# Two transformer layers on one core: first shifted copies on GpSimd, and a planner that models the shared SBUF port

## The chip, the core and the metric

The program runs on one core of one Trainium2 chip. A core has five engines with a queue each: TensorE (PE, matmuls, with its weight loads shown apart as PEld), VectorE (DVE), ScalarE (ACT), GpSimd (POOL) and SyncE (SP, which issues the DMAs here). Each engine takes its instructions in the order of its queue; between engines semaphores set the order. The metric is the device time of one execution in microseconds (us), lower is better. The median of three executions is compared.

## What is computed

Input is x, 1 x 2048 x 512 in bfloat16. An attention block with 32 heads of 16 channels and a dense block with 1792 hidden channels are applied, then both a second time with the same weights.

```python
def _A_ref(x, wqkv, wo):
    qkv = (x @ wqkv).reshape(B, S, 3, H, Dh).transpose(2, 0, 3, 1, 4)
    q, k, v = qkv[0], qkv[1], qkv[2]
    scores = jnp.einsum("bhqd,bhkd->bhqk", q, k) * (Dh ** -0.5)
    p = _softmax(scores, axis=-1)
    o = jnp.einsum("bhqk,bhkd->bhqd", p, v)
    return o.transpose(0, 2, 1, 3).reshape(B, S, D) @ wo

def _B_ref(x, w1, b1, w2, b2):
    h = _gelu(jnp.einsum("bsd,df->bsf", x, w1) + b1)
    return jnp.einsum("bsf,fd->bsd", h, w2) + b2

x = x + _A_ref(_layernorm(x), A_wqkv, A_wo)
x = x + _B_ref(_layernorm(x), B_w1, B_b1, B_w2, B_b2)
x = x + _A_ref(_layernorm(x), A_wqkv, A_wo)
x = x + _B_ref(_layernorm(x), B_w1, B_b1, B_w2, B_b2)
```

The exponentials are the bulk of the elementwise work: 2 layers x 32 heads x 2048 x 2048 scores.

## The kernel before

**Cells.** The scores are made in cells of 128 keys x 512 columns of (query, head), one PSUM bank each. There are 4096 cells. They are grouped in passes: a pass is one layer, one chunk of 512 queries (a "segment"; the last chunk of layer 1 is cut in two), one group `g` of heads, and a list of key tiles. In a pass with all 16 key tiles there are 64 cells, since each key tile has four cells `a`, one for each 32-row group of TensorE.

**Two ways to take an exponential.** Most cells go to ScalarE, which reads two or three PSUM banks in one Exp (line 1466, `exps`). The cells of four key tiles of each layer (`KD`, line 45) may go to VectorE instead; let us call such a cell a d-cell. For a d-cell `dfirst` (line 1283) turns the score into a 16-bit integer whose bits are, read as bfloat16, a coarse power of two. To make the power accurate, the sum over four copies is used, whose integers are shifted by 0, 32, 64 and 96. They are weighted by copies of V that GpSimd has scaled (`VC`, line 1068, weights `VW`). So a d-cell takes four PV matmuls (one with V, three with VC) where a cell of ScalarE takes one.

**The chain of a pair.** d-cells are evacuated into a buffer `du`, which holds two of them (four buffers), one of them (one buffer, `dh` in the trace), or two in a piece of `kt` that is free in layer 1. When both cells of a buffer are in, `dchain` (line 1332) makes the shifted copies: line 1344 makes copy 1 from copy 0 for all cells of the buffer at once (the first shifted copy, 128 x 1024 for two cells), and line 1346 makes copies 2 and 3 from copies 0 and 1 (the second shifted copy, 128 x 2048). Both are VectorE instructions here, and they read and write SBUF. Then the PV matmuls read the four copies, and the buffer is free again.

**Who gets a d-cell.** `attach` (line 1215) adds d-cells to a matmul group that makes scores for ScalarE. It needs a free bank (6 or 7, which the projections and the dense layers use as well), a free `du` buffer, and a bank whose last reader will be done in time. `swap` (line 1192) gives a bank of ScalarE's own to VectorE when VectorE is not more than 0.5 us behind. `solo` (line 1291) makes one alone. Whatever d-cells are left when a pass has no others go to ScalarE (`next_act`). So the number of d-cells isn't fixed: it is what the planner finds room for.

**The planner.** Everything else follows from a list scheduler written in the kernel (`_Sched`, lines 208 to 390), which runs when the program is built. Each step of work is an `_Op` with an engine and a price in us. Generators (threads with a priority) yield ops, and ask for slots of named pools (`acq`, `take`, `rel`). The planner keeps a clock for each engine, picks the op that can start first (or, among ready ones, the one of the best priority), and appends it to its engine's queue. So the order in every queue is fixed when the program is built, from these prices; on the chip only the semaphores move the work. A thread's code between two ops runs as soon as the op before has been placed.

**Around the change.** `norm` (line 718) ends a pass: it adds the parts, transposes the sums to `XT`, takes the reciprocal of the row sums to `RC`, multiplies to `OTT` (on GpSimd for most passes, line 754) and transposes back to `OTN`. `passes` (line 1003) sets the order of passes: in layer 1 the first chunk's eight passes and `EARLY` passes of the second chunk run first over 12 key tiles, and then over the last 4, whose keys come from the last chunk of layer 0. A pass cut in two needs a copy (line 734) and an add (line 739) of VectorE in place of one transpose from PSUM. `free` (line 1090) chooses a PSUM bank for filler matmuls[...], among banks 0 to 7; bank 5 (`PVB`) collects the PV sums. GpSimd otherwise makes masked queries (`qpad`, line 1085), layer norm outputs (line 602), reciprocal roots (line 588) and VC.

Of the kernel before, what the change touches and what calls it, by code (L numbers as in the profile page):

```python
# [5 lines left out]
ALU = mybir.AluOpType  # L6
# [25 lines left out]
DU = 9  # L32
# [8 lines left out]
PACE = {(1, 2): (0.03, 0.05, 0.36, 0.02), (1, 3): (0.05, 0.07, 0.55, 0.1)}  # L41
JB = 0.64
JS = 0.025
EARLY = 4
KD = ((4, 5, 6, 7), (0, 1, 2, 12))
NKD = 4
TAIL = 10
# [12 lines left out]
COLD = 8  # L60
DPRIO = 9
CPRIO = 8
FPRIO = 1.5
PVP = 2
PTURG = 6
# [9 lines left out]
SHIFT = 32  # L75
# [126 lines left out]
        self.done = False  # L202


LATENCY = {"pe": 0.20, "act": 0.10, "dve": 0.10, "pool": 0.15, "sp": 0.1}


class _Sched:
# [5 lines left out]
    def __init__(self, P):  # L214
        self.P = P
        self.clock = {e: 0.0 for e in P.ENGS}
        self.end = {}
        self.pools = {}
        self.tokens = {}
        self.threads = []  # L220
        self.nseq = 0
        self.mode = "F"
        self.ops = []
        self.stream = []
        self.filler, self.free, self.fills = None, None, set()

    def pool(self, name, slots):
        self.pools[name] = list(slots)
# [66 lines left out]
    def _prio(self, op):  # L295
        return op.prio() if callable(op.prio) else op.prio

    def landed(self, keys):
        return max(self.end.get(self.P.lastw[k], 0.0) if k in self.P.lastw else 1e9 for k in keys)

# [33 lines left out]
    def run(self):  # L334
        while True:
            moved = True
            while moved:
                moved = False
                for th in list(self.threads):
                    if self._advance(th):  # L340
                        moved = True
            self.threads = [t for t in self.threads if not t.done]
            best = {}
            for th in self.threads:
                if th.op is None:
                    continue
                e = th.op.eng
                rdy = self._ready(th.op)
                if rdy is None:
                    continue  # L350
                best.setdefault(e, []).append((th, rdy))
            if not best:
                if self.threads:
                    raise RuntimeError("stuck: %r" % [(t.prio, t.block) for t in self.threads])
                return
            pick = None
            for e, cand in best.items():
                now = self.clock[e]
                nowc = [c for c in cand if c[1] <= now]
                if nowc:  # L360
                    ch = min(nowc, key=lambda c: (self._prio(c[0].op), c[0].seq))
                else:
                    ch = min(cand, key=lambda c: (c[1], self._prio(c[0].op), c[0].seq))
                start = max(now, ch[1])
                stop = start + self._cost(ch[0].op)
                for c in cand:
                    if c[0].op.slack is not None and c is not ch and c[1] + c[0].op.slack < stop:
                        ch = c
                        start = max(now, ch[1])
                        break  # L370
                if pick is None or start < pick[0]:
                    pick = (start, e, ch[0])
            start, e, th = pick
            op = th.op
            th.op = None
            if op.late is not None:
                op.late(op, start)
            if e == "pe":
                mode = self.mode
                self.fill(start, op)  # L380
                if mode != self.mode:
                    start = max(self.clock["pe"], start - SW * (op.mode != self.mode) + SW * (op.mode != mode))
            ev = self.P.group(e, op.fns, op.reads, op.writes, op.sem, op.by)
            cost = self._cost(op)
            if e == "pe":
                self.mode = op.mode
                self.note(start + cost - op.cost, start + cost, op)
            self.ops.append((e, start, cost, op.writes[0] if op.writes else ""))
            self.clock[e] = start + cost
            self.end[ev] = start + cost + op.tail + LATENCY[e]  # L390

# [110 lines left out]
class _Plan:  # L502
# [215 lines left out]
    def norm(self, l, seg, g, b, part, final):  # L718

        T = self.T  # L720
        pv = self.bank(b)
        key = "B.%d" % b
        qc, q0, w = seg
        if qc == 0:
            pt, pk = T["PART"][l][:, g, :], "PART.%d.%d" % (l, g)
            over = ["V0.%d" % k for k in range(self.NT)] + ["V01"] if l else []
        else:
            pt, pk = T["PART1"][:, g, :], "PART1.%d" % g
            over = ["K0.%d.%d" % (g // 2, c) for c in range(self.NQ)]
        prev = self.before(l, seg)  # L730
        if final and prev:
            yield ("need", ("ofree",) + prev)
        if not final:
            yield _Op("dve", DV, lambda e: e.tensor_copy(pt, pv), reads=[key], writes=[pk] + over)
            yield ("rel", "pv", b)
            return
        xt = T["XT"]
        if part:
            yield _Op("dve", DV, lambda e: e.tensor_tensor(out=pt, in0=pt, in1=pv, op=ALU.add), reads=[key, pk], writes=[pk])
            yield ("rel", "pv", b)  # L740
            yield _Op("dve", 0.7, lambda e: e.transpose(xt[:, :], pt), reads=[pk], writes=["XT"])
        else:
            yield _Op("dve", 0.7, lambda e: e.transpose(xt[:, :], pv), reads=[key], writes=["XT"])  # L743
            yield ("rel", "pv", b)
        x3 = xt[:, :].rearrange("p (k c) -> p k c", c=32)
        yield _Op("dve", 0.23, lambda e: e.reciprocal(T["RC"][:, :].rearrange("p (k o) -> p k o", o=1), x3[:, :, 16:17]),  # L746
                  reads=["XT"], writes=["RC"])
        gb, ts = self.heads(seg, g)
        o = gb % 2
        pool = g < 6 and seg[2] == 512  # L750
        nb = w // 32
        for i, t in enumerate(ts):
            o3 = T["OTT"][:, o, 0:w].rearrange("p (k c) -> p k c", c=32)[:, :, 16 * t:16 * t + 16]
            yield _Op(*(("pool", 0.1 + 0.55 * w / 512) if pool else ("dve", 0.1 + 0.31 * w / 512)), lambda e, i=i, o3=o3: e.tensor_tensor(  # L754
                out=o3, in0=x3[:, i * nb:i * nb + nb, 0:16],
                in1=T["RC"][:, i * nb:i * nb + nb, None].to_broadcast([128, nb, 16]), op=ALU.mult),
                reads=["XT", "RC"], writes=["OTT.%d.%d" % (o, t)])
        if ts[-1] == 1:
            yield _Op("dve", 0.05 + 0.65 * w / 512, lambda e: e.transpose(T["OTN"][:, gb, q0:q0 + w], T["OTT"][:, o, 0:w]),
                      reads=["OTT.%d.0" % o, "OTT.%d.1" % o],  # L760
                      writes=["OTN.%d.%d" % (gb, t % 4) for t in self.tiles(seg)])
            yield ("give", ("otn", l, seg, gb))

    def heads(self, seg, g):
# [325 lines left out]
    def free(self, now, ahead):  # L1090
        P = self.P
        best = (None, 1e9)
        src = self.source()
        for b in (6, 7, 0, 1, 2, 3, 4, 5) if src else ():
            k = "B.%d" % b
            if k in ahead or b in self.hold or k in P.lastw and not P.reads.get(k) and P.lastw[k] not in self.s.fills:
                continue
            t = max([0.0] + [self.s.end.get(ev, 0.0) + FOLD for ev in P.deps(src, [k]) if ev[0] != "pe"])
            if max(t, now) < max(best[1], now):
                best = (b, t)  # L1100
        k = "B.%d" % PVB
        if best[1] > now and self.pvopen and "VC.0.0" in P.lastw and k not in ahead:
            best = (PVB, 0.0)
        return best
# [227 lines left out]
    def dchain(self, pair):  # L1332
# [5 lines left out]
        if self.open is pair:  # L1338
            self.open = None
        yield ("cond", lambda: pair.get("done", 0) == len(cells))  # L1340
        n = len(cells)
        U = T["DU"][du]
        key = [["DU.%d.%d.%d" % (du, i, j) for j in range(n)] for i in range(4)]
        yield _Op("dve", 0.08 + 0.14 * n, lambda e: e.tensor_scalar(U[:, 1, 0:n, :], U[:, 0, 0:n, :], SHIFT, None, op0=ALU.add),  # L1344
                  reads=key[0], writes=key[1])
        yield _Op("dve", 0.08 + 0.28 * n, lambda e: e.tensor_scalar(U[:, 2:4, 0:n, :], U[:, 0:2, 0:n, :], 2 * SHIFT, None, op0=ALU.add),  # L1346
                  reads=key[0] + key[1], writes=key[2] + key[3])
        self.duleft[du] = n
        for jj, (pi, kt, a) in enumerate(cells):
            l, seg, g = self.pas[pi][:3]  # L1350
            gb, ts = self.heads(seg, g)
# [208 lines left out]
    def run(self):  # L1560
        s = self.s
        self.phase = {}
        s.pool("misc", MISC)
        s.pool("dbank", [])
        s.route = self.route
        s.pool("pv", [PVB])
        s.pool("s", range(len(SLOTS)))
# [54 lines left out]
```

The softmax here doesn't subtract the row's maximum and nothing guards it: scores larger than these inputs give would overflow.

## Time and profile before

| What | Value |
|---|---|
| median of three executions | 1588.41 us (1587.63 to 1589.98) |
| the profiled execution | 1589.16 us, span of its instructions 1587.3 us |
| granted TensorE clock, mean | 0.995 |
| GpSimd busy | 200.5 us in 250 instructions |
| cells on ScalarE / on VectorE | 3207 / 889 |
| first shifted copies | 391 of two cells, 107 of one cell |
| first Exp starts, last Exp ends | 12.6 us, 1560.8 us |

The cells are counted from the forms of lines 1466 and 1283. A row of a group gives its line, engine and operation, what it writes and reads, its shapes and count, its busy time in us, the mean of one in ns, and the idle time of the engine just before it with what ended most of that. Busy time is a union: overlapping instructions count once. In a table by stretches of time, the count in brackets stands beside the busy us of each engine.

### The profile page before, as it was taken

The numbers are of one execution on the slowest core, as the hardware profiler recorded it, in microseconds if no ns is written. First come the engines' busy times: TensorE is split into PE (matmuls) and PEld (weight loads), VectorE is DVE, ScalarE is ACT, GpSimd is POOL, SyncE is SP. The second block draws the span as 40 slices with busy tenths as digits, with TensorE's granted clock in tenths as the row PEclk, the third lists the DMA queues.
The fourth block names the chain that finished last, engine by engine and source line by source line (L and its number), as shares of the span: only waits on it lengthen the run. The fifth ranks groups of instructions, "written<-read, shape, count | busy, mean of one in ns | idle before, by whom it ended". The sixth has DMA issues, their size and how long they took to land.

```text
span 1587.3 us, 42896 instructions
## 1 busy us (share of the span) xinstructions
PE 1424.2 (90%) x18701; PEld 444.6 (28%) x18701; DVE 1352.0 (85%) x2564; ACT 1547.1 (97%) x1393; POOL 200.5 (13%) x250
## 2 busy tenths in 40 slices
PE   8998888899999898988989998888998889898988
PEld 3222222222222222222222222222222222333344
DVE  5689999888898889978788789899878988998984
ACT  7999999999999999999999999999999999999996
POOL 5200012001100201002120020122001000010000
PEclk9999999999999999999999999999999999999999
DMA  5100001241114311143111510001251105312520
GB/s 140 22 2 1 2 14 41 77 132 46 27 45 130 85 41 28 42 140 74 36 28 48 172 44 28 1 2 33 67 167 43 28 15 151 103 36 87 155 82 29
DMA packets 141767, 96.88 MB, mean 61 GB/s; under 512 B 36877, under 2 KB 141582, under 8 KB 141582
## 3 DMA queue, kind: packets, MB, share of 16 engines
q1 hardware_dynamic: 141582, 94.14, 21.2%
q8 instruction: 149, 2.44, 0.6%
q14 instruction: 36, 0.29, 0.1%
HBM read 84.41 MB, written 2.10 MB: 55 GB/s over the span
## 4 chain that ended last, share of the span: by engine, by line
ACT 67%; PE 29%; DVE 2%; POOL 1%; issue 1%; DMA 0%; ACTq 0%; POOLq 0%
ACT pt L1466 60%; PE ps L512 11%; PE ps L1137 9%; PE ps L1527 8%; ACT g L893 3%; ACT v L1466 2%; ACT kt L1466 1%; ACT q L1466 1%; DVE du L1283 1%; ACT L893 1%; ACT L1466 0%; DMA xf<-xln 0%; PE ps L1125 0%; POOL xln L602 0%; POOL rstd L588 0%
## 5 line engine op out<-in xcount | busy, mean ns | idle before, releaser
L1466 ACT ACTIVATE pt<-ps 128x1536 bf16<-128x1536 f32 (+2 forms) x1261 | 1384.2, 1246 | 15.2 <-PE ps L1137 10.3
L1137 PE MATMUL ps<-qp,kt 32*128 32x512 bf16 x4096 | 538.0, 385 | 140.8 <-ACT pt L1466 106.7
L1283 DVE TENSOR_SCALAR du<-ps 128x512 uint16<-128x512 f32 x711 | 479.7, 685 | 97.5 <-PE ps L1137 89.6
L1527 PE MATMUL ps<-pt,v 128*17 128x512 bf16 (+1 forms) x3368 | 433.8, 359 | 2.3 <-ACT pt L1466 0.8
L1527 PE MATMUL ps<-du,vc 128*17 128x512 bf16 (+1 forms) x2394 | 333.8, 358 | 2.7 <-DVE du L1346 1.4
L1137 PEld LDWEIGHTS ps<-qp,kt 32*128 32x128 bf16 x4096 | 140.6, 91 | 685.9 <-ACT pt L1466 304.2
L1346 DVE TENSOR_SCALAR du<-du 128x2048 uint16<-128x2048 uint16 x361 | 246.3, 687 | 2.5
L1085 POOL TENSOR_SCALAR qp<-q,mask 128x512 bf16<-128x512 bf16 (+1 forms) x91 | 66.3, 728 | 1013.8 <-PE ps L1137 1005.1
L512 PE MATMUL ps<-xf,wr 128*32 128x512 bf16 (+1 forms) x2400 | 170.8, 368 | 1.7 <-DMA xf<-xln 1.1
L1527 PE MATMUL ps<-du,v 128*17 128x512 bf16 (+1 forms) x798 | 154.7, 360 | 1.7 <-DVE xt L743 0.9
L1344 DVE TENSOR_SCALAR du<-du 128x1024 uint16<-128x1024 uint16 x361 | 150.5, 428 | 2.0
L1527 PEld LDWEIGHTS ps<-pt,v 128*17 128x17 bf16 x3368 | 111.8, 89 | 113.0 <-issue 72.9
L512 PE MATMUL ps<-wr,g 128*32 128x512 bf16 x1600 | 123.8, 384 | 5.5 <-ACT g L893 5.0
L1527 PEld LDWEIGHTS ps<-du,vc 128*17 128x17 bf16 x2394 | 92.5, 89 | 62.7 <-issue 27.5
L872 DVE TENSOR_SCALAR g<-ps,hb1t 128x512 bf16<-128x512 f32 (+1 forms) x112 | 79.8, 713 | 13.8 <-PE ps L512 12.9
L1527 PE MATMUL ps<-dh,vc 128*17 128x512 bf16 (+1 forms) x321 | 90.6, 358 | 0.0
L1283 DVE TENSOR_SCALAR dh<-ps 128x512 uint16<-128x512 f32 x96 | 65.8, 685 | 11.5 <-PE ps L1137 10.8
L1283 DVE TENSOR_SCALAR kt<-ps 128x512 uint16<-128x512 f32 x82 | 56.1, 684 | 20.7 <-PE ps L1137 19.9
L512 PEld LDWEIGHTS ps<-xf,wr 128*32 128x32 bf16 x2400 | 53.6, 95 | 61.5 <-issue 33.5
L602 POOL TENSOR_SCALAR xln<-x,rstd,nmr 128x512 bf16<-128x512 bf16 x58 | 58.2, 1008 | 33.3 <-DMA xf<-xln 23.2
L754 POOL TENSOR_TENSOR ott<-xt,rc 128x256 bf16<-128x256 f32 x42 | 29.5, 703 | 178.5 <-DVE rc L746 178.5
L1125 PE MATMUL ps<-vc 128*32 128x512 bf16 x476 | 50.9, 395 | 0.1
(93 smaller groups left out, 1185.2 us busy)
## 6 DMA issues: line engine op xcount, KB each, us to landing
wr<-in_B_w_dram SPq DMA_DIRECT2D x256, 256.0 KB, 2.9
wr<-in_A_wqkv_dram SPq DMA_DIRECT2D x24, 256.0 KB, 2.9
wr<-in_A_wo_dram SPq DMA_DIRECT2D x18, 256.0 KB, 2.9
out_dram<-x SPq DMA_DIRECT2D x16, 128.0 KB, 2.7
g<-in_A_wqkv_dram SPq DMA_DIRECT2D x3, 512.0 KB, 5.1
x<-in_A_x_dram SPq DMA_DIRECT2D x3, 512.0 KB, 8.0
q<-in_B_w_dram SPq DMA_DIRECT2D x3, 512.0 KB, 3.9
kt<-in_B_w_dram SPq DMA_DIRECT2D x4, 256.0 KB, 3.3
```

Of the source, the lines that this page charges most:

```text
L512: return [lambda e, a=a: e.matmul(out[32 * a:32 * a + 32, :], lhsT=lhsT[:, 32 * a:32 * a + 32], rhs=rhs, start=start, stop=stop, tile_posi ...
L602: yield _Op(eng, cost, lambda e: e.tensor_scalar(T["XLN"][:, x, :], T["X"][:, t, :], T["RSTD"][:, t:t + 1], T["NMR"][:, t:t + 1], op0=ALU. ...
L872: yield _Op("dve", 0.21 + n / 966, lambda e, fc=fc, pb=pb: e.tensor_scalar(T["G"][:, fc, q], pb, T["HB1T"][:, fc:fc + 1], None, op0=ALU.ad ...
L893: lambda e, g=g: e.activation(out=g, in_=g, func=ACT.Gelu_apprx_tanh), reads=gk, writes=gk, prio=2)
L1085: yield _Op("pool", 0.1 + 0.6 * w / 512, lambda e, s=s, q=q, i=i, t=t, w=w: e.tensor_scalar(T["QP"][:, s, w * i:w * i + w], q, T["MASK"][: ...
L1125: fns.append(lambda e, o=o, w=w, a=a, m=m: e.matmul(o, lhsT=w, rhs=rhs, start=start, stop=start, tile_position=(0, m * a)))
L1137: return (lambda e: e.matmul(o, lhsT=lhsT, rhs=rhs, start=True, stop=True, tile_position=(32 * a, 0)), ["K%d.%d.%d" % (l, gb, kt // 4), "Q ...
L1283: yield _Op("dve", 0.68, lambda e: e.tensor_scalar(u, self.bank(b), E_SCALE, E_BIAS, op0=ALU.mult, op1=ALU.add), reads=["B.%d" % b], write ...
L1344: yield _Op("dve", 0.08 + 0.14 * n, lambda e: e.tensor_scalar(U[:, 1, 0:n, :], U[:, 0, 0:n, :], SHIFT, None, op0=ALU.add), reads=key[0], w ...
L1346: yield _Op("dve", 0.08 + 0.28 * n, lambda e: e.tensor_scalar(U[:, 2:4, 0:n, :], U[:, 0:2, 0:n, :], 2 * SHIFT, None, op0=ALU.add), reads=k ...
L1466: yield _Op("act", 0.065 + 0.4267 * n, lambda e, src=src, dst=dst: e.activation(out=dst, in_=src, func=ACT.Exp, scale=0.25), reads=["B.%d" ...
L1527: op.fns.append(lambda e, o=o, lhsT=q[0][0][m], rhs=q[0][1][:, n * m:n * m + n], a=a, st=st, sp=sp: e.matmul(o, lhsT=lhsT, rhs=rhs, start= ...
```

## The change

The first shifted copy of a buffer goes to GpSimd if, when its last evacuation has been placed, GpSimd's clock in the plan is less than `SPARE` = 0.3 us past VectorE's; else VectorE makes it as before. The planner prices it at 0.1 us + 0.65 us for each cell there. The second copy stays on VectorE (`WHOLE` is False). The planner also keeps the last four stretches in which each of the two engines holds the port to SBUF that they share: on GpSimd every op but the reciprocal root, on VectorE the shifted copies and the quick layer norm output. `unlocked` moves an op's ready time to the end of such a stretch of the other engine, unless VectorE follows closely on a locking op of its own.

Four edits come with it. `EARLY` goes from 4 to 2. `norm` takes a slot for `XT` and for its half of `OTT`, and gives them back when they have been read. Bank 5 is no longer in the list that `free` runs over (it still takes zero-weight fillers by the rule below that list). The prices of other ops are as before.

```diff
-EARLY = 4
+EARLY = 2
...
+SPARE = 0.3
+WHOLE = False
...
+HOLD = (0.05, 0.13)
...
+    def locking(self, op):
+        w = op.writes[0] if op.writes else ""
+        if op.eng == "pool":
+            return not w.startswith("RSTD")
+        return op.eng == "dve" and (w.startswith("XLN") or w.startswith("DU") and w.split(".")[2] != "0")
+
+    def unlocked(self, op, rdy):
+        if op.eng not in self.locks or not self.locking(op):
+            return rdy
+        now = t = max(rdy, self.clock[op.eng])
+        for a, b in self.locks["pool" if op.eng == "dve" else "dve"]:
+            if a <= t < b and not (op.eng == "dve" and a >= self.fast[0] and t < self.fast[1] + 0.02):
+                t = b
+        return t if t > now else rdy
...
-                best.setdefault(e, []).append((th, rdy))
+                best.setdefault(e, []).append((th, self.unlocked(th.op, rdy)))
...
+            if self.locking(op):
+                self.fast = (start, start + cost) if e == "dve" else self.fast
+                self.locks[e] = self.locks[e][-3:] + [(start + HOLD[0], start + cost - HOLD[1])]
...
+        gb, ts = self.heads(seg, g)
+        yield ("acq", "xt")
         if part:
...
+        if ts[0] == 0:
+            yield ("take", ("ott", o))
...
+        yield ("rel", "xt", 0)
         if ts[-1] == 1:
...
+            yield ("rel", "ott", o)
...
-        for b in (6, 7, 0, 1, 2, 3, 4, 5) if src else ():
+        for b in (6, 7, 0, 1, 2, 3, 4) if src else ():
...
-        yield _Op("dve", 0.08 + 0.14 * n, lambda e: e.tensor_scalar(U[:, 1, 0:n, :], U[:, 0, 0:n, :], SHIFT, None, op0=ALU.add),
+        clock = self.s.clock
+        eng, fix, one = ("pool", 0.1, 0.65) if clock["pool"] < clock["dve"] + SPARE else ("dve", 0.08, 0.14)
+        yield _Op(eng, fix + one * n, lambda e: e.tensor_scalar(U[:, 1, 0:n, :], U[:, 0, 0:n, :], SHIFT, None, op0=ALU.add),
                   reads=key[0], writes=key[1])
-        yield _Op("dve", 0.08 + 0.28 * n, lambda e: e.tensor_scalar(U[:, 2:4, 0:n, :], U[:, 0:2, 0:n, :], 2 * SHIFT, None, op0=ALU.add),
+        eng, fix, one = ("pool", 0.1, 0.65) if eng == "pool" and WHOLE else ("dve", 0.08, 0.14)
+        yield _Op(eng, fix + 2 * one * n, lambda e: e.tensor_scalar(U[:, 2:4, 0:n, :], U[:, 0:2, 0:n, :], 2 * SHIFT, None, op0=ALU.add),
                   reads=key[0] + key[1], writes=key[2] + key[3])
```

More of the change, by code (lines that the diff above doesn't have):

```diff
@@ L225, in __init__ @@
         self.filler, self.free, self.fills = None, None, set()
+        self.locks = {"pool": [], "dve": []}
+        self.fast = (0.0, 0.0)
     def pool(self, name, slots):
@@ L747, in norm @@
                   reads=["XT"], writes=["RC"])
-        gb, ts = self.heads(seg, g)
         o = gb % 2
+        if ts[0] == 0:
+            yield ("take", ("ott", o))
         pool = g < 6 and seg[2] == 512
@@ L1564, in run @@
         s.pool("dbank", [])
+        s.pool("xt", [0])
+        s.pool("ott", [0, 1])
         s.route = self.route
```

## The prediction

> **What bounds the kernel now.** I read the busy line first, then the chain of waits, the groups, and last the table of stretches of 40 us.
>
> ```profile
> span 1587.3 us, 42896 instructions
> PE 1424.2 (90%) x18701; PEld 444.6 (28%) x18701; DVE 1352.0 (85%) x2564; ACT 1547.1 (97%) x1393; POOL 200.5 (13%) x250
> ...
> ACT 67%; PE 29%; DVE 2%; POOL 1%; issue 1%; DMA 0%; ACTq 0%; POOLq 0%
> ...
> L1466 ACT ACTIVATE pt<-ps 128x1536 bf16<-128x1536 f32 (+2 forms) x1261 | 1384.2, 1246 | 15.2 <-PE ps L1137 10.3
> ```
>
> ScalarE is busy 97% of the span, and in front of its main row of Exps it idled 15.2 us in all. First Exp to last is 12.6 to 1560.8 us; what lies outside (a start, and a tail of 26.5 us on the last dense block) isn't touched by the change. So the time falls only if ScalarE gets fewer cells, or rises if it has to wait. Its 1547.1 us less everything that isn't Exp on scores (gelu 43.9 + 3.3, table loads 10.3 + 9.0 + 1.3, casts and others 13.8) leave 1465.5 us for 3207 cells: 0.457 us a cell. Each cell that VectorE takes in addition is worth that much.
>
> What then limits VectorE's share, 889 cells of the 1024 that its key tiles hold?
>
> ```profile
> 160.00:200.00 40.00, 32.41 (x364) 8.74 (x363) 37.77 (x74) 39.99 (x36) 3.02 (x4) 1.00 0.01 2
> 680.00:720.00 40.00, 35.78 (x470) 11.00 (x470) 27.63 (x50) 39.88 (x32) 1.34 (x3) 1.00 0.53 154
> 880.00:920.00 40.00, 36.72 (x483) 10.88 (x485) 30.17 (x53) 39.80 (x37) 1.39 (x2) 1.00 0.55 158
> 1240.00:1280.00 40.00, 35.12 (x439) 10.20 (x437) 37.61 (x69) 39.87 (x37) 2.94 (x4) 1.00 0.08 21
> ```
>
> The columns are PE, PEld, DVE, ACT, POOL busy. There are two kinds of stretch. Where dense work is thin, VectorE is busy 37 to 38 of 40 us: it is full. Where weights stream (DMA share 0.5) it is busy 28 to 30, and TensorE and the two banks shared with the dense layers set the limit. Of the 38 stretches from 40 to 1560 us, 23 have VectorE at 35 us or more: 60%. GpSimd is nearly idle in both kinds.
>
> ```profile
> L1283 DVE TENSOR_SCALAR du<-ps 128x512 uint16<-128x512 f32 x711 | 479.7, 685 | 97.5 <-PE ps L1137 89.6
> L1346 DVE TENSOR_SCALAR du<-du 128x2048 uint16<-128x2048 uint16 x350 | 241.2, 693 | 2.5
> L1344 DVE TENSOR_SCALAR du<-du 128x1024 uint16<-128x1024 uint16 x350 | 147.9, 433 | 2.0
> L1085 POOL TENSOR_SCALAR qp<-q,mask 128x512 bf16<-128x512 bf16 x75 | 56.4, 752 | 854.6 <-PE ps L1137 846.6 <-ACT q L669 7.9
> ```
>
> With the smaller forms, the first copies (L1344) are 195 us, the second ones (L1346) 317 us and the evacuations 889 x 0.685 = 609 us. A d-cell costs VectorE 1.26 us. I also paired each copy with its evacuations in the order of the records: from the end of the last evacuation to the start of the first copy a chain waits 3.0 us in the median (3.5 mean), since evacuations go first, and from the first copy's end to the second's start 0.64 us. Buffers stand full in that wait.
>
> **What the Trainium skill says.** "SBUF — State Buffer", section "Who interferes with whom": GpSimd shares a pair of ports with VectorE's two-port modes, and whoever starts first holds it for the whole instruction while the other blocks. The trace agrees; at 190.97 us a GpSimd op started first, and a copy that has 684 ns in the median took 1.05 us:
>
> ```profile
> 190.97 0.69 POOL L1085 TENSOR_SCALAR qp<-q,mask 128x512 bf16<-128x512 bf16 x1 [8.42 <-PE ps L1137]
> ...
> 191.15 1.05 DVE L1346 TENSOR_SCALAR du<-du 128x2048 uint16<-128x2048 uint16 x1
> ```
>
> "VectorE: DVE Perf Modes", section "The perf-mode tier table": a 16-bit tensor_scalar in SBUF runs at 4x, 693 ns for 2048 elements, and PSUM sources run slower. Our rows have 693 for 2048 and 685 for 512 from PSUM, so the copies are two-port and the evacuations, which overlap GpSimd without getting longer (690 ns either way), are not. "GPSIMD Engine Reference", section 4.1: one-input elementwise work is roughly line rate there. Undisturbed, line 1085 has 694 ns for 512 elements and 482 for 256, so 0.83 ns an element.
>
> **The change, part by part.**
>
> First copies that move. A buffer goes to GpSimd unless GpSimd is booked over 0.3 us past VectorE. Chains start 3.0 us apart in the mean, a quarter of the gaps under 0.8 us; a copy books 1.4 us, and GpSimd's other work holds 13%. I estimate that 65% go: 254 of the 391 pairs and 70 of the 107 singles. That takes 254 x 0.43 + 70 x 0.28 = 129 us from VectorE. EARLY = 2 takes two pairs of copy and add, 4 x 0.69 = 2.7 us more.
>
> Their price on GpSimd. No row has a 16-bit integer add there. From below: line 1068 has 646 ns undisturbed for 544 elements, so 646 + 480 x 0.83 = 1.04 us for 1024. From above: two of line 1085 with its disturbances, 1.50 us, and more if integers are converted in more steps. I take the planner's 1.4 us (0.75 for one cell), as it lies inside. GpSimd gets 254 x 1.4 + 70 x 0.75 = 408 us, so about 610 us, 38%. Queued behind such a copy are qpad, layer norm outputs and OTT products; they are made for passes ahead or for work with a pass's length of slack (about 25 us), so 1.4 us there costs nothing. If that cover fails, it is 1.4 us on a chunk's dense block, some ten times.
>
> The port. Now 36 of the 996 copies are over 0.12 us longer than their median, 13 us in excess. With GpSimd busy three times as long, ops 1.6 times as long, and 670 two-port copies left of 996, this gives 13 x 3 x 1.6 x 0.67 = 42 us for a plan blind to the port, and nothing if the plan evades every clash. I take 20.
>
> New d-cells. Net relief is 129 + 3 - 20 = 112 us. A d-cell then costs 0.685 + 0.357 + about 0.09 = 1.13 us, so 99 cells if VectorE were the only limit. It is in 60% of the time: 60 cells. In the other stretches banks and TensorE hold, and I take a third of the remaining 39: 13. So 73 cells, within the 135 left. Gain on ScalarE: 73 x 0.457 = 33 us. The copy's wait of 3.0 us also goes, for about 0.2 + 1.4 us on GpSimd, so buffers come free no later than now.
>
> What they add. 3 more PV matmuls for each, 219 in all, beside 944 filler matmuls (two rows of L1125, 476 and 468) that exist only to fill TensorE's gaps; they replace those. But VectorE's and GpSimd's queues now wait on each other, and a late copy delays evacuations behind it, then the scores' bank, then an Exp. ScalarE's waits could stay at 15.2 us or double; I take 10 more.
>
> EARLY also takes 2 x 48 cells out of the stretch that covers the last chunk's keys of layer 1. The last of them (L683) lands at 953 us, and the passes over them would start at cell 2528, which was scored at 972 us: 19 us in hand, so nothing; if the cover were gone, ScalarE would wait for as much as is missing. XT and OTT slots bind passes 25 us apart, and the removed bank is one of eight for fillers: nothing each.
>
> Sum: -33 + 10 = -23, and 1589.2 - 23 = 1566 for the profiled execution. The median shown is 0.8 us below that execution: 1565.
>
> **Rivals.** (a) Forecast: 15 to 80 more d-cells, 1579 to 1546; chance 0.62. (b) The freed time turns idle, because banks, buffers and TensorE limit d-cells everywhere: evacuations already idle 97.5 us waiting for TensorE, which speaks for it; VectorE at 37.8 of 40 us speaks against. 10 more cells less 5 us of waits: 1588; chance 0.15, half of it within 0.2%. (c) Nearly all 135 cells go over, with no more waits: 1589 - 135 x 0.457 = 1527, or 1540 for 105; needs the dense stretches to gain as well; 0.07. (d) Slower: the GpSimd copy takes longer than planned. The second copy stands in VectorE's fixed queue and waits for it, with all evacuations behind. In full stretches there are 324 x 0.6 = 195 such chains; the 0.64 us that now lie between the copies cover half, so each us of mean lateness costs 97 us. Against the 23 us gained it decides from 0.24 us, a pair's copy of 1.64 us. At 1.8 us it costs 39 us: 1589 - 23 + 39 = 1605. For it speaks that no trace shows the integer op there; against it the undisturbed 0.83 ns an element. Chance 0.16, one part of it within 0.2%. That the change does nothing is excluded by GpSimd's idleness, which meets its condition at almost any time.
>
> **Numbers.** A measurement here can tell 0.2%, 3 us, from no change. Faster: 0.62 + 0.08 + 0.07 = 0.77; same 0.08; slower 0.15. The range leaves 0.06 below 1545 (c) and some 0.13 above 1592 (d).
>
> **What would show it.** Right: some 320 tensor_scalar adds on GpSimd near 1.4 us (1.1 for clean ones); 940 to 980 evacuations of line 1283; Exp time down about 33 us; ACT still at 96 to 97%; second copies with few over 0.9 us; d-cells up in the full stretches and little elsewhere. Wrong: a GpSimd copy of 1.7 us or more, VectorE idle before second copies with GpSimd as the releaser, or d-cells up and ScalarE's share down by as much.

## The result and the profile after

| | before | after |
|---|---|---|
| median of four | 1588.66 us | 1881.16 us |
| ratio, 95% interval | | 1.184 (1.182 to 1.186) |
| d-cells, of 4096 cells | 889 | 927 |
| first copies on GpSimd | 0 of 498 | 492 of 519 |
| granted TensorE clock | 0.995 | 0.929 |

The kernel became 18% slower; 1565 us was forecast. The page after, in the order used before: busy time, the chain of waits, the groups that matter.

```profile
span 1879.3 us, 43405 instructions
PE 1535.6 (82%) x18877; PEld 448.0 (24%) x18877; DVE 1365.2 (73%) x2148; ACT 1560.4 (83%) x1388; POOL 1488.6 (79%) x740
...
POOL 59%; DVE 23%; PE 15%; issue 1%; ACT 1%; DMA 0%; SPq 0%; DVEq 0%
...
L1497 ACT ACTIVATE pt<-ps 128x1024 bf16<-128x1024 f32 (+1 forms) x1257 | 1393.9, 1195 | 271.0 <-PE ps L1165 254.2
```

ScalarE was 67% of the chain and is 1%; GpSimd was 1% and is 59%. ScalarE now idles 271 us in front of the Exps where it idled 15. Its busy time is 13 us longer although it has 38 cells fewer. Before, the durations of its Exps, added one by one, are 1669 us, and the time that they cover is 1467 us: back to back they overlap. After they add to 1599 and cover 1480, since the waits leave less to overlap. ScalarE is idle for 318.9 us of the span against 40.2, which is 279 us more. These 279 and the 13 are the whole 292 us.

The groups by form show why: the GpSimd copies, and VectorE's second copies, which were 693 ns.

```profile
L1374 POOL TENSOR_SCALAR du<-du 128x1024 uint16<-128x1024 uint16 x360 | 1025.3, 2857 | 245.6 <-DVE du L1311 240.4 <-DVE varr L609 4.1
L1374 POOL TENSOR_SCALAR dh<-dh 128x512 uint16<-128x512 uint16 x79 | 129.3, 1636 | 13.6 <-DVE dh L1311 13.5
...
L1377 DVE TENSOR_SCALAR du<-du 128x2048 uint16<-128x2048 uint16 x366 | 348.1, 958 | 194.3 <-POOL du L1374 193.8
```

A copy of 1024 elements takes 2.86 us in the mean (2.77 in the median), where the planner has 1.40 and my bounds were 1.04 and 1.50. VectorE idles 194 us in front of this group of second copies for GpSimd, and each takes 265 ns longer than before. GpSimd's own queue, from the timeline, shows that the delay adds up:

```profile
599.51 5.50 POOL L1374 TENSOR_SCALAR du<-du 128x1024 uint16<-128x1024 uint16 x2 [1.41 <-DVE du L1311]
604.98 1.62 POOL L1374 TENSOR_SCALAR dh<-dh 128x512 uint16<-128x512 uint16 x1
606.57 2.76 POOL L1374 TENSOR_SCALAR du<-du 128x1024 uint16<-128x1024 uint16 x1
```

Three copies of two cells and one of a single cell follow without a gap, 9.8 us of work that the plan has as 4.95. On VectorE in the same stretch:

```profile
605.05 1.09 DVE L1377 TENSOR_SCALAR du<-du 128x2048 uint16<-128x2048 uint16 x1 [0.62 <-POOL du L1374]
606.63 1.25 DVE L1377 TENSOR_SCALAR dh<-dh 128x1024 uint16<-128x1024 uint16 x1 [0.50 <-POOL dh L1374]
607.80 0.68 DVE L1311 TENSOR_SCALAR du<-ps 128x512 uint16<-128x512 f32 x1
609.37 0.69 DVE L1377 TENSOR_SCALAR du<-du 128x2048 uint16<-128x2048 uint16 x1 [0.89 <-POOL du L1374]
```

Each second copy first stands in the queue until its first copy is done, and the first two then take far longer than their 0.69 and 0.43 us, because the next GpSimd copy has begun. The evacuation at 607.80, with its bank of scores, comes after both. That is the rival (d) of the prediction, at a size it didn't have. In all, VectorE idles 291 us waiting for GpSimd, where it idled 2.4 us before.

The lines show one thing more. The second copy at 606.63 began 0.06 us after a GpSimd copy and ended 1.45 us before it: GpSimd did not hold the port for the whole of its 2.76 us. A second copy that began later in a GpSimd copy wasn't held up at all:

```profile
1436.56 2.77 POOL L1374 TENSOR_SCALAR du<-du 128x1024 uint16<-128x1024 uint16 x1
...
1437.53 0.68 DVE L1377 TENSOR_SCALAR du<-du 128x2048 uint16<-128x2048 uint16 x1
```

I take the GpSimd copies of two cells in this trace that were not delayed themselves. The 61 second copies that began in the first 0.1 us of one took 0.81 to 0.89 us longer than normal. The 20 that began between 0.9 and 1.7 us into one took no longer than normal. In the run `e2_priced` below, 13 that began 1.8 to 2.5 us into one were held again, until 2.63 to 2.67 us after its start. So the prediction's sentence, that whoever starts first holds the port "for the whole instruction", does not fit the slow copy, and the planner, which books the port for nearly the whole of a copy, has it wrong there. For the fast copy of `e5_mult_add` below it nearly fits: six second copies were held until 0.91 us after the start of a copy of 1.05 us.

### The profile page after: what moved, and what is told of

It is laid out like the page before. It is cut to its first block, busy times and chain, and to the rows that moved or that the text cites. A ratio compares the mean times of both kernels' runs of the same rounds, so it can differ in the third digit from the quotient of the medians.

```text
span 1879.3 us, 43405 instructions
## 1 busy us (share of the span) xinstructions
PE 1535.6 (82%) x18877; PEld 448.0 (24%) x18877; DVE 1365.2 (73%) x2148; ACT 1560.4 (83%) x1388; POOL 1488.6 (79%) x740
## 4 chain that ended last, share of the span: by engine, by line
POOL 59%; DVE 23%; PE 15%; issue 1%; ACT 1%; DMA 0%; SPq 0%; DVEq 0%
POOL du L1374 44%; DVE du L1311 7%; DVE du L1377 7%; PE ps L535 6%; POOL kt L1374 4%; PE ps L1558 4%; POOL dh L1374 4%; PE ps L1165 4%; POOL qp L1113 2%; POOL xln L625 2%; DVE g L900 1%; ACT pt L1497 1%; DVE kt L1311 1%; DVE dh L1377 1%; POOL ott L780 1%
## 5 line engine op out<-in xcount | busy, mean ns | idle before, releaser
L1497 ACT ACTIVATE pt<-ps 128x1024 bf16<-128x1024 f32 (+1 forms) x1257 | 1393.9, 1195 | 271.0 <-PE ps L1165 254.2
L1374 POOL TENSOR_SCALAR du<-du 128x1024 uint16<-128x1024 uint16 (+1 forms) x370 | 1041.6, 2824 | 247.0 <-DVE du L1311 241.8
L1165 PE MATMUL ps<-qp,kt 32*128 32x512 bf16 x4096 | 556.8, 405 | 178.3 <-DVE du L1311 86.7
L1377 DVE TENSOR_SCALAR du<-du 128x2048 uint16<-128x2048 uint16 (+1 forms) x379 | 356.7, 949 | 196.8 <-POOL du L1374 196.2
L1558 PE MATMUL ps<-pt,v 128*17 128x512 bf16 (+1 forms) x3317 | 478.1, 379 | 26.3 <-POOL du L1374 9.7
L1558 PE MATMUL ps<-du,vc 128*17 128x512 bf16 (+1 forms) x2511 | 375.6, 390 | 35.5 <-DVE du L1377 18.7
L1374 POOL TENSOR_SCALAR kt<-kt 128x1024 uint16<-128x1024 uint16 (+1 forms) x43 | 119.3, 2775 | 29.3 <-DVE kt L1311 29.2
L1374 POOL TENSOR_SCALAR dh<-dh 128x512 uint16<-128x512 uint16 x79 | 129.3, 1636 | 13.6 <-DVE dh L1311 13.5
L900 DVE TENSOR_SCALAR g<-ps,hb1t 128x512 bf16<-128x512 f32 (+1 forms) x112 | 79.1, 706 | 10.5 <-PE ps L535 10.3
L1377 DVE TENSOR_SCALAR dh<-dh 128x1024 uint16<-128x1024 uint16 x96 | 61.8, 644 | 18.9 <-POOL dh L1374 18.8
L1558 PE MATMUL ps<-kt,vc 128*17 128x512 bf16 (+1 forms) x324 | 60.7, 371 | 5.3 <-DVE du L1377 3.2
```

Source lines behind the costliest of these rows:

```text
L900: yield _Op("dve", 0.21 + n / 966, lambda e, fc=fc, pb=pb: e.tensor_scalar(T["G"][:, fc, q], pb, T["HB1T"][:, fc:fc + 1], None, op0=ALU.ad ...
L1165: return (lambda e: e.matmul(o, lhsT=lhsT, rhs=rhs, start=True, stop=True, tile_position=(32 * a, 0)), ["K%d.%d.%d" % (l, gb, kt // 4), "Q ...
L1374: yield _Op(eng, fix + one * n, lambda e: e.tensor_scalar(U[:, 1, 0:n, :], U[:, 0, 0:n, :], SHIFT, None, op0=ALU.add), reads=key[0], write ...
L1377: yield _Op(eng, fix + 2 * one * n, lambda e: e.tensor_scalar(U[:, 2:4, 0:n, :], U[:, 0:2, 0:n, :], 2 * SHIFT, None, op0=ALU.add), reads=k ...
L1497: yield _Op("act", 0.065 + 0.4267 * n, lambda e, src=src, dst=dst: e.activation(out=dst, in_=src, func=ACT.Exp, scale=0.25), reads=["B.%d" ...
L1558: op.fns.append(lambda e, o=o, lhsT=q[0][0][m], rhs=q[0][1][:, n * m:n * m + n], a=a, st=st, sp=sp: e.matmul(o, lhsT=lhsT, rhs=rhs, start= ...
```

## Experiments: what makes the copy slow

Two questions were open. Why does the copy take 2.77 us, when other tensor_scalar rows on GpSimd have 0.83 ns an element? And is the loss the slow copy as such, or a plan made with half its price? The first batch:

`e1_two_ops`, the copy as two additions on GpSimd:

```diff
-tensor_scalar(U[:, 1, 0:n, :], U[:, 0, 0:n, :], SHIFT, None, op0=ALU.add)
+tensor_scalar(U[:, 1, 0:n, :], U[:, 0, 0:n, :], SHIFT, 0.0, op0=ALU.add, op1=ALU.add)
```

> The changed kernel, with the GpSimd copy written as two operations (add 32, add 0) instead of one; same plan, same order of every queue. In the changed kernel the copy of 1024 elements took 2.77 us in the median, 2.5 ns an element, where the planner has 1.40; the two-operation rows on bfloat16 have 0.83 ns an element. Theory A (the form with one operation is what is slow): the copy falls to 1.0 to 1.3 us and the kernel to 1560 to 1575 us, since the plan is then kept. Theory B (16-bit integers are slow on GpSimd): the copy stays at 2.7 us or gets longer, the kernel stays at 1880 us or above.

`e4_bf16_view`, the same bytes as bfloat16:

```diff
-tensor_scalar(U[:, 1, 0:n, :], U[:, 0, 0:n, :], SHIFT, None, op0=ALU.add)
+tensor_scalar(U[:, 1, 0:n, :].bitcast(BF16), U[:, 0, 0:n, :].bitcast(BF16), SHIFT, None, op0=ALU.add)
```

> The changed kernel, with the GpSimd copy (one operation, as it is) reading and writing the same bytes as bfloat16 instead of uint16, so that copy 1 holds other values; only its time is of interest. Theory A (one-operation form slow): still 2.5 ns an element, 2.7 us. Theory B (integer type slow): 0.8 to 0.9 ns an element, 1.0 to 1.2 us for 1024, and the kernel at 1560 to 1580 us.

Measured: two additions 2217.4 us (ratio 1.397, 1.394 to 1.399), the copy 3.63 us in the median (the 3.67 in the texts below is the mean). The bfloat16 view, one execution: 1885.7 us. Its row, from the view of the buffer's tile (shortest, median and longest in ns):

```profile
L1375 POOL TENSOR_SCALAR du<-du x370: 1485/2770/3581, 68.5 to 1847.2; 128x1024 bf16<-128x1024 bf16 x177, 128x512 bf16<-128x512 bf16 x8
```

To the nanosecond the same median as with uint16. So theory B, the integer type, is out, and theory A in its form of then ("one operation is slow, two are fast") is out as well: a second addition made it slower. What is left is the kind of operation. The fast rows of before are line 1085 (times mask, times 1.0), line 1068 (times weight, times 1.0) and line 602 (times, plus): two operations, at least one of them a multiplication. Line 602 has a single form, 0.77 us for 512 elements, so its time for one element isn't known, though the first text below counts it in. Three runs separate the number of operations, the multiplication and its place. `e5_mult_add` has

```diff
-tensor_scalar(U[:, 1, 0:n, :], U[:, 0, 0:n, :], SHIFT, None, op0=ALU.add)
+tensor_scalar(U[:, 1, 0:n, :], U[:, 0, 0:n, :], 1.0, SHIFT, op0=ALU.mult, op1=ALU.add)
```

on GpSimd, `e6_mult_alone` has `1.0, None, op0=ALU.mult`, and `f4_add_mult` has `SHIFT, 1.0, op0=ALU.add, op1=ALU.mult`. In all of them, and in the two runs above, each queue has the same instructions in the same order as in the changed kernel, since the planner's prices aren't touched.

> The changed kernel, plan and queues as they are, with the GpSimd copy written as times 1.0, plus 32 in place of plus 32. One add took 2.77 us for 1024 elements, on uint16 and on the same bytes as bfloat16 alike, and two adds 3.67 us; the rows on GpSimd that begin with a multiplication (masked queries, scaled V, layer norm outputs) have 0.83 ns an element. Theory E (it is the pair of operations that decides: multiply first is fast, add first is slow): the copy takes 1.0 to 1.25 us, below the planner's 1.40, and the kernel 1560 to 1580 us, faster than before. Theory F (anything on these buffers is slow on GpSimd, by place or integer values): 2.8 us or more, the kernel at 1880 us or above.

> As the run with times 1.0, plus 32, but with the multiplication by 1.0 alone, so that copy 1 holds what copy 0 holds; only its time is of interest. If one operation alone is slow as such, the copy takes 2.7 us here and the kernel 1880 us; if the add as first operation is what is slow, it takes 1.0 to 1.25 us and the kernel 1560 to 1580 us.

> As the run with times 1.0, plus 32, with the two operations the other way round: plus 32, times 1.0; same values. If it is a multiplication as first operation that is fast on GpSimd, this takes over 2.7 us a copy (two adds took 3.67 us) and the kernel 1880 us or more. If any pair with a multiplication is fast, it takes 1.05 us and the kernel 1584 us.

The row of the copy with times 1.0, plus 32, and then that of times 1.0 alone:

```profile
L1375 POOL TENSOR_SCALAR du<-du x370: 616/1047/1522, 68.2 to 1548.1; 128x1024 uint16<-128x1024 uint16 x177, 128x512 uint16<-128x512 uint16 x8
```

```profile
L1375 POOL TENSOR_SCALAR du<-du x370: 1485/2770/3577, 68.6 to 1843.0; 128x1024 uint16<-128x1024 uint16 x177, 128x512 uint16<-128x512 uint16 x8
```

| operations on GpSimd | 1024 elements, median us | kernel, us |
|---|---|---|
| plus 32 (the change) | 2.77 | 1881.2 |
| plus 32, on bfloat16 | 2.77 | 1885.7 (one execution) |
| times 1.0 | 2.77 | 1880.8 (one execution) |
| plus 32, plus 0 | 3.63 | 2217.4 |
| times 1.0, plus 32 | 1.05 | 1584.3 |
| plus 32, times 1.0 | 1.05 | 1580.2 (one execution) |

A pair with a multiplication in either place takes 1.05 us, one operation alone 2.77, two additions 3.63. So theory E has the right time for times 1.0, plus 32, but not the right reason: the single multiplication is as slow as the single addition, and the order of the pair makes no difference. The kernel with that pair is also 4 us above the 1560 to 1580 us that the theory gave it. From the undisturbed forms of 512 and 1024 elements, the pair has (1047 - 621) / 512 = 0.83 ns an element, one operation (2770 - 1489) / 512 = 2.50, two additions (3628 - 1921) / 512 = 3.33. Why a pair with a multiplication is faster was not found out, and other operations or other constants than 1.0 weren't run in the copy.

With the pair, the same queues that gave 1881 us give 1584.3 us: ratio 0.9967 to the kernel before (0.9957 to 0.9977). So in this plan the duration of this one instruction is the whole loss, and the rest of the change, the move to GpSimd included, gains a little.

## Experiments: the plan, and the other edits

`e2_priced` leaves the slow copy and tells the planner its price.

```diff
-eng, fix, one = ("pool", 0.1, 0.65) if clock["pool"] < clock["dve"] + SPARE else ("dve", 0.08, 0.14)
+eng, fix, one = ("pool", 0.22, 1.275) if clock["pool"] < clock["dve"] + SPARE else ("dve", 0.08, 0.14)
```

> The changed kernel, with the planner's price for the GpSimd copy set to what was measured (0.22 + 1.275 us a cell, 2.77 us for two) and nothing else. Theory C (the time was lost because the plan was made with a price of half: queues in the wrong order): the kernel falls to 1590 to 1630 us, waits of ScalarE for scores from 271 to under 60 us, and the d-cells fall below 889. Theory D (the shared port itself costs it, whatever the plan): the second copies on VectorE stay at 950 ns, and the kernel stays above 1750 us.

It ran in 1633.5 us (ratio 1.028, 1.027 to 1.030), 3.5 us above the range of theory C and far below that of theory D. The busy time of the engines, and the groups of the second copies and of the main Exps, by form:

```profile
PE 1457.4 (89%) x18809; PEld 451.7 (28%) x18809; DVE 1285.4 (79%) x2134; ACT 1568.7 (96%) x1401; POOL 1075.3 (66%) x573
```

```profile
L1377 DVE TENSOR_SCALAR du<-du 128x2048 uint16<-128x2048 uint16 x336 | 272.5, 821 | 14.6 <-POOL du L1374 14.4
```

```profile
L1497 ACT ACTIVATE pt<-ps 128x1024 bf16<-128x1024 f32 x749 | 786.1, 1091 | 4.9 <-PE ps L1165 2.6 <-PE ps L1558 1.7
L1497 ACT ACTIVATE pt<-ps 128x1536 bf16<-128x1536 f32 x506 | 765.3, 1512 | 28.4 <-PE ps L1558 15.2 <-PE ps L1165 11.1
```

The copies are as slow as ever, yet VectorE waits 15 us for them instead of 194, and ScalarE 33 us instead of 271. The second copies are down from 958 to 821 ns, so the port costs less in this plan too, though not nothing (693 before). The plan finds 844 d-cells, 45 fewer than before; ScalarE's busy time is 21.6 us longer than before (45 x 0.457 = 21), and its idle time 22.3 us longer. So of the 292 us, 248 go when the price in the plan is true, with the instruction unchanged. But this plan also sends only 325 copies to GpSimd in place of 492. How much of the 248 us comes from the order of the queues, and how much from a third fewer slow copies, wasn't separated.

`e7_mult_add_priced` does the reverse: the fast pair, and the planner's price lowered from 1.40 to the undisturbed time.

```diff
-eng, fix, one = ("pool", 0.1, 0.65) if clock["pool"] < clock["dve"] + SPARE else ("dve", 0.08, 0.14)
+eng, fix, one = ("pool", 0.2, 0.43) if clock["pool"] < clock["dve"] + SPARE else ("dve", 0.08, 0.14)
```

> Times 1.0, plus 32 as before, with the planner's price for it set to 0.2 + 0.43 us a cell (1.06 us for two), the undisturbed figure of line 1068 taken to 1024 elements. Theory E: the copy at that time, chains shorter, 15 to 40 more d-cells than before, 1560 to 1580 us and within 6 us of the run that keeps the old price. Theory F: slower than the run with the old price, since the plan is then further from the chip.

1599.8 us, ratio 1.0067 (1.0046 to 1.0087): slower than with the price that is too high, and outside what theory E expected. Theory F has the direction right, but not its reason: the copies of two cells take 1.11 us in the mean. This plan has 906 d-cells, not 927. In the profiled executions, 1592.9 us against 1586.1 with the old price, the cells account for all of it: ScalarE is busy 8.5 us longer (21 x 0.457 = 10), and idle 1.7 us less. VectorE does idle longer before the second copies, 25.6 us against 10.5, but that did not reach ScalarE there. The other half of the 15 us between the medians goes with a lower granted clock: four of the six executions had 0.981 to 0.986 and took 1598.0 to 1603.6 us, the two with 0.991 took 1592.9 and 1595.7, and those of `e5_mult_add` with 0.991 took 1585.6 and 1585.9. Whether this plan brings the lower clock about isn't shown.

The other edits. `e3_all_dve` is the change with `SPARE = -1e9`, so that no copy moves. `f1_all_dve_early4` has `EARLY = 4` besides. `k1_slots_bank` also takes the port out of the planner (`locking` returns False for both engines).

> The changed kernel with SPARE = -1e9, so that no copy goes to GpSimd; EARLY = 2, the slots for XT and OTT, the bank list and the port in the planner stay. If the GpSimd copies are the whole loss, this is at the time before, 1583 to 1594 us (my steps for the four other edits were nothing and 3 us of VectorE). If one of them costs (keys of the last chunk late at EARLY = 2, above all), it is 1600 us or more.

> No copy on GpSimd (as the run with SPARE = -1e9, 1594.7 us, 0.37% above before) and EARLY back at 4. If EARLY = 2 is what cost those 6 us, this is at the time before, 1586 to 1591 us. If the port in the planner, the slots or the bank list cost them, it stays at 1593 to 1597 us.

> No copy on GpSimd, EARLY = 4 and the port out of the planner: of the change only the slots for XT and OTT and the bank list are left. With the port this was 1597.4 us, 0.46% above before. If the planner's port cost those 8 us, this is at the time before, 1586 to 1592 us. If the slots or the bank list cost them, 1594 to 1600 us; the number of d-cells hardly tells, 885 here against 889.

| no copy on GpSimd, and | median us | ratio to before |
|---|---|---|
| EARLY 2, port, slots, bank list | 1594.7 | 1.0037 (1.0025 to 1.0048) |
| EARLY 4, port, slots, bank list | 1597.4 | 1.0046 (1.0029 to 1.0064) |
| EARLY 4, slots, bank list | 1595.2 | 1.0043 (1.0029 to 1.0056) |

All three are 6 to 8 us above before. Neither EARLY nor the port accounts for it. What the three share are the slots for XT and OTT and the shorter bank list, which I had at nothing. These two weren't run apart, and part of it may be that any edit reshuffles the plan (885 d-cells for 889 is 2 us).

With the fast copies the same two parts matter, in the other direction. `f2_mult_add_early4` is the fast pair with `EARLY = 4`, `f3_mult_add_nolock` the fast pair with the port out of the planner.

> Times 1.0, plus 32 on GpSimd at the planner's old price, with EARLY back at 4. If EARLY = 2 costs 6 us, this beats the 1584.3 us of the run with EARLY = 2 by about that: 1576 to 1581 us. If EARLY is neutral, it is at 1582 to 1588 us, since this plan finds fewer cells for VectorE (915 instead of 927, 12 x 0.457 = 5 us).

> Times 1.0, plus 32 on GpSimd, EARLY = 2, but with the port left out of the planner: no op is moved for it. My step took 20 us of longer copies on VectorE for a plan that knows the port and 42 us for one that doesn't. If that holds, second copies go from 762 ns in the mean to 800 ns or more, and the kernel from 1584 to 1590 to 1600 us. If the planner's port does nothing on the chip, both stay, within 4 us.

They ran in 1592.1 and 1597.7 us. The ratios to before are 1.0016 (1.0008 to 1.0023) and 1.0048 (1.0031 to 1.0064), against 0.9967 with both parts in. So the plan with EARLY = 2 is about 0.5% faster than that with EARLY = 4, where I had expected it to cost or to be neutral. This is one pair of plans, the slower of which has 12 d-cells fewer (5 us), and without copies on GpSimd the same step made no clear difference; that EARLY = 2 gains as such isn't shown. The plan with the port is 0.8% faster than that without, with 927 d-cells in both. In the profiled executions ScalarE is idle for 61.9 us without the port and 51.8 with it. The second copies without the port in the plan, then with it (fast pair in both):

```profile
L1378 DVE TENSOR_SCALAR du<-du 128x2048 uint16<-128x2048 uint16 x369 | 288.9, 790 | 19.2 <-POOL du L1375 19.2
```

```profile
L1378 DVE TENSOR_SCALAR du<-du 128x2048 uint16<-128x2048 uint16 x366 | 274.4, 762 | 10.5 <-POOL du L1375 10.4
```

28 ns for each and 9 us of waits: 19 us of VectorE in this group, beside my 22 us (42 less 20) for the difference. The mean stayed under the 800 ns that I expected. The sizes themselves were larger than mine: beyond 0.684 and 0.418 us for the two forms, all second copies together took 42 us with the port in the plan and 57 without, where before they took 6.

## Why the prediction was wrong

**The step that failed** is "Their price on GpSimd". It read "From above: two of line 1085 with its disturbances, 1.50 us", and took the planner's 1.4 us because it lay between the bounds. The copy takes 2.77 us, and with this the forecast of 1565 us became 1881. Both bounds were made from rows of another form: lines 1068 and 1085 multiply twice, the copy adds once. Their second multiplication, by 1.0, changes no value, and that it stands in lines which could do without it was to be seen in the code. The prediction did say "No row has a 16-bit integer add there", but looked for the risk in the type, which e4 shows to cost nothing. The page "GPSIMD Engine Reference", section 4.1, has one-input work at roughly line rate; the measured 2.50 ns an element is three times the 0.83 that the trace of before gave for a pair with a multiplication.

**The rival (d)** had the right mechanism, a late copy that holds up VectorE's fixed queue. Its size was wrong. "each us of mean lateness costs 97 us" would give 1589 - 23 + 1.37 x 97 = 1699 us for 2.77 us. Three runs with the same queues give larger slopes: 1584.3 us at 1.05, 1881.2 at 2.77, 2217.4 at 3.63. If nothing is lost up to the planned 1.40, an assumption, since no run lies between 1.05 and 2.77, that is 297 / 1.37 = 217 us per us up to the changed kernel; it is 336 / 0.86 = 391 beyond it. Its threshold, "from 0.24 us, a pair's copy of 1.64 us", wasn't tested, and under that assumption it is too high: a gain of 4 us in place of 23 is used up 0.02 us past 1.40. Two of its terms were too small. I counted 195 chains; 492 have their copy on GpSimd. And I let the 0.64 us between the copies cover half, as if each chain were late by itself; on a GpSimd that is 79% busy one late copy makes the next one late, as the timeline shows.

Two other steps of the prediction had their part in the loss. The longer second copies, 20 us in the step "The port" (for 324 copies of 1.4 us), came to 138 us by the count above, since in a backlog a second copy is let go just when the next GpSimd copy starts. And the cover for what stands behind a copy, "so 1.4 us there costs nothing", failed: of the 291 us that VectorE waited for GpSimd, 54 were for reciprocal roots and OTT products.

**Which copies move**: I estimated 65% of 498, it is 95% of 519. The rule compares with the clock of VectorE, which I take to be booked as far ahead as GpSimd nearly always; that isn't shown.

**What held, once the copy has the time it was given.** In e5 the copy takes 1.05 us, my lower bound of 1.04, and the sum can be read. ScalarE's busy time and the Exps' waits there:

```profile
PE 1429.7 (90%) x18877; PEld 445.2 (28%) x18877; DVE 1277.2 (81%) x2148; ACT 1532.5 (97%) x1388; POOL 716.4 (45%) x740
```

```profile
L1498 ACT ACTIVATE pt<-ps 128x1024 bf16<-128x1024 f32 x797 | 820.4, 1075 | 10.4 <-PE ps L1165 9.1
L1498 ACT ACTIVATE pt<-ps 128x1536 bf16<-128x1536 f32 x459 | 692.4, 1508 | 13.5 <-PE ps L1165 7.4 <-PE ps L1559 4.8
```

ScalarE's busy time falls by 14.6 us for 38 cells, 0.38 us each (I had 0.457), and its idle time in the span rises from 40.2 to 51.8 us, 11.6 us (I had 10). The term that is too large is the number of cells: 73 expected, 38 found, although VectorE was relieved of more than I reckoned (its first copies fell from 199 to 13 us, where I took 129 us off). I took VectorE to be the limit in the 23 stretches where it was busy 35 us or more. More time did not help there: the evacuations that start in these stretches went from 577 to 587, where I had 60 more, and in the other 15 from 312 to 340, where I had 13. Much of the freed time stands idle: in the 23 stretches VectorE is busy 796 of 920 us instead of 841, and in front of the evacuations it waits longer for the scores of TensorE. The row of the main ones, which had 97.5 us in the prediction:

```profile
L1311 DVE TENSOR_SCALAR du<-ps 128x512 uint16<-128x512 f32 x745 | 502.0, 685 | 131.0 <-PE ps L1165 126.2
```

That is the rival (b) in large part. Whether banks, TensorE's time or the planner's rules hold the cells back wasn't separated. So even with the copy at its lower bound the forecast of 1565 would have been missed by 19 us; the sign would have been right, and 1584 lies between the 1545 and 1592 of the prediction.

**A sum of the forecast** doesn't come out: 15 to 80 more cells at 0.457 us, with 10 us of waits or none, give 1592 to 1552 us, not 1579 to 1546.

**The other edits** were costed at nothing. Without copies on GpSimd they are 6 us slower. That 19 us in hand for the last chunk's keys suffice agrees with EARLY = 4 not being faster in either pair of runs.

## What to carry to other kernels

Price an operation on GpSimd from a row with the same operations, not only the same instruction name and shape; if there is none, measure it by itself before a planner is given its price. In a kernel whose queues are ordered ahead of time, a price that is too low can cost more than the slow instruction: here 248 of 292 us went when the plan was told the truth, which also made it use the instruction less. That a price above the undisturbed time did better than the undisturbed time is one pair of plans and no rule. And an engine that is busy over 90% of a stretch need not be the only limit there: 23 such stretches of VectorE gained 10 cells when it was relieved, not 60.

## What wasn't expected of the hardware

In these runs tensor_scalar on GpSimd takes 2.50 ns an element with one operation, an addition on uint16 or bfloat16 or a multiplication by 1.0 on uint16; 3.33 with two additions; and 0.83 with an addition and a multiplication, in either order. So the longer instruction is the faster one: adding "times 1.0" takes a 1024-element copy from 2.77 to 1.05 us and this kernel from 1881 to 1584 us.

The slow copy does not hold the port for all of its time: a second copy that starts with it loses 0.83 us, one that starts 0.9 to 1.7 us into it loses nothing, although the GpSimd copy runs for 2.77 us.

While the queues waited on GpSimd, the granted TensorE clock fell as well, from 0.995 to 0.929 in the changed kernel and 0.843 with two additions, and was 0.990 with the fast pair. The queues are the same in these three, so the lower clock came with the slow copy; how much of the time it cost wasn't measured apart.
